# Integer additions moved to VectorE, the first block's second product in float32, and an elu without ScalarE's ReLU

## The chip, the cores and the metric

The kernel runs on one core of a Trainium2 chip. The metric is the device time in microseconds (us) of one execution. A core has five engines that run side by side, each through its own instructions in a fixed order: TensorE (PE; its weight loads are shown as PEld), VectorE (DVE), ScalarE (ACT), GpSimd (POOL) and SyncE (SP), which here only issues DMAs. Engines wait for each other through semaphores, and an instruction that waits holds up all that stand behind it on its engine.

## The reference

Three stages follow each other: a local and block attention, a feed-forward layer with elu, and a mixture of experts.

```python
x = attention(q, k, v)                  # 1536 tokens x 512
h = x @ w_in                            # w_in 512 x 2048
g = where(h > 0, h, exp(min(h, 0)) - 1) # elu
x = g @ w_out                           # w_out 2048 x 512
logits = x @ w_gate                     # 8 experts, the largest is taken
out[mask] = gate * eom * (relu(x[mask] @ w1[e]) @ w2[e])
```

The change touches only the middle lines: how w_in and w_out are converted, how elu is computed, and how `g @ w_out` is multiplied for the first tokens.

## The kernel before

**Blocks and chunks.** The 1536 tokens are worked in four blocks of 512, 256, 384 and 384 tokens (`UNITS`, in units of 64). For each block j the feed-forward layer goes through 16 chunks c of 128 of its 2048 inner columns. `mm_h` makes h of chunk c in a PSUM bank (twelve matmuls, L422), `elu` makes g from it, and `mm_y` adds g times the chunk's rows of w_out into the block's y (L467, one output tile for each 128 tokens). A step of the loop in `part1` emits `mm_h` of its chunk, then `elu`, then `mm_y` of the chunk two steps back, so on PE the order is h of c, y of c-2, h of c+1, y of c-1, h of c+2, y of c.

**Two forms of a product.** In most chunks both factors are split into a high and a low part of type float32r and multiplied with three matmuls for a tile: `split_w` makes the parts of w_out (`wsp`: a cast on ACT at L175, a subtraction on DVE at L176), `split_g` those of g (`gh` on ACT at L447, `gl` on DVE at L448). In the first block's chunks below `C3` (8 before) both splits are left out, and one matmul in float32 stands for a tile (each shows as two matmul records).

**Elu.** `elu` has two instructions of ACT on h, tanh(h/2) into `elt` (L433) and exp(h) into `ele` (L434), and a third, the ReLU of h into `elp` (L435). DVE then makes (exp + 1) * tanh, which is exp(h) - 1, at L436, and min(that, 0) + ReLU at L437. The PSUM banks of h come from the pool `psh`, which has two: h of chunk c+2 can start only when the last reader of h of chunk c is through.

**Conversion.** The weights w_in and w_out come as 64 bit numbers in 32 pieces (16 chunks, two weights each), and the kernel turns each into float32: `conv_r` on ACT rounds the lower word (L127), `conv_t` makes the float's bits from the upper word with two instructions of DVE (L138, L139), and `conv_f` adds the two as integers on POOL (L146). For w_in a split follows: `conv_h` on ACT (L152) and `conv_l`, a subtraction on DVE, or on POOL for three of the sixteen chunks (`LOE`, L157). Seven pieces are converted in `start_up`, whose order is written out in `START`; the other 25 are converted during the first block, two for each step.

**What sets the order.** Apart from `start_up` and the last stage, a scheduler orders each engine's instructions by its own costs and priorities. The attention of a later block's units (L309 to L405) is worked in between the chunks. The pools `gp` (`gh`, `gl`), `ws` and `stg` are rings of a few buffers.

Of the kernel before, what the change touches and what calls it, by code (L numbers as in the profile page):

```python
# [9 lines left out]
F32 = mybir.dt.float32  # L10
# [4 lines left out]
AF = mybir.ActivationFunctionType  # L15
ALU = mybir.AluOpType
# [19 lines left out]
BLK = [j for j in range(NBLK) for _ in range(UNITS[j])]  # L36
NF = FF // 128
NS = 6
C3 = 8
WARM = 22  # L40
AT0 = (2, -2, 1)
ATS = (5, 4, 5)
# [14 lines left out]
EXD = (3, 5)  # L57
EXP = (0, 1, 2, 3, 4, 6, 7)
NORMD = (0, 4, 7)
LOE = "VVVPVV"  # L60
START = "w23 w43 x3 w53 w03 w13 w33 w51 x1 w31 w21 w11 w41 w01 w52 x2 w22 w02 w12 w42 w50 x0 w00 w20 w32 d2 d0 w40 d5 k2 s0 w30 d3 k4 k1 k3 s2 k0 k5 m0 w10 s5 m2 e0 s3 m5 M0 e2 m3 d4 M1 r0 b5 d1 b3 s4 n0 e5 r2 t0 e3 m4 n2 s1 c0 z3 e4 M2 z5 t2 r3 r5 M3 n3 c2 m1 A00 M4 n5 B00 e1 M5 k6 r4 C00 n4 t5 P s6 r1 c5 p1 n1 A01 p6 t4 p2 D0 o5 B01 c4 o2 h5 k7 m6 t3 C01 h2 s7 c3 E0 e6 t1 p7 m7 p0 A10 r6 o0 c1 p3 n6 p4 e7 o3 l5 B10 o1 t6 h3 r7 h0 C10 l3 c6 n7 o4 A11 l0 h1 t7 B20 h4 o6 A20 c7 l1 C20 h6 l4 o7 D1 l2 l6 H0 h7 E1 D2 l7 A30 B30 E2 C30 H1 B11 C11 D3 A21 B21 E3 C21"
HID = (5, 10, 15)
LOP = (1, 3, 5, 8, 10, 12, 14)
# [16 lines left out]
class Prog:  # L80
# [60 lines left out]
    def conv_f(self, c, part):  # L141
        t2, r = self.cv.pop((c, part))
        f = t2
        if part == 1:
            f = self.wo[:, c].bitcast(I32)
        self.nc.gpsimd.tensor_tensor(f, t2, r, op=ALU.add)  # L146
        self.w[c, part] = f

    def conv_h(self, c):
# [4 lines left out]

    def conv_l(self, c):
        w, f = self.w[c, 0], self.cvf.pop(c)
        (self.nc.gpsimd if LOE[c % len(LOE)] == "P" else self.nc.vector).tensor_tensor(w[:, 1], f, w[:, 0].bitcast(F32), op=ALU.subtract)  # L157

    def conv_a(self, c, part):
        self.conv_r(c, part)  # L160
# [8 lines left out]
    def split_w(self, j, c):  # L169
        if j == 0 and c < C3:  # L170
            return
        nc = self.nc
        f = self.w[c, 1].bitcast(F32)
        w = self.ws.tile([128, 2, 512], F32R, tag="ws", name="wsp")
        nc.scalar.copy(w[:, 0], f)  # L175
        nc.vector.tensor_tensor(w[:, 1], f, w[:, 0].bitcast(F32), op=ALU.subtract)  # L176
        self.wsp[j, c] = w
# [247 lines left out]
    def elu(self, j, c):  # L425
        nc = self.nc
        h = self.h.pop((j, c))
        t = self.el.tile([128, TB], F32, tag="t", name="elt", bufs=1)[:, :TBS[j]]
        e = self.el.tile([128, TB], F32, tag="e", name="ele", bufs=1)[:, :TBS[j]]

        pool, tag = (self.gp, "gh" if c % 2 else "gl") if j == 0 and c < C3 else (self.el, "p")
        p = pool.tile([128, TB], F32, tag=tag, name="elp")[:, :TBS[j]]
        nc.scalar.activation(t, h, AF.Tanh, scale=0.5)  # L433
        nc.scalar.activation(e, h, AF.Exp)  # L434
        nc.scalar.activation(p, h, AF.Relu)  # L435
        nc.vector.scalar_tensor_tensor(t, e, 1.0, t, op0=ALU.add, op1=ALU.mult)  # L436
        nc.vector.scalar_tensor_tensor(p, t, 0.0, p, op0=ALU.min, op1=ALU.add)  # L437
        self.g[j, c] = p

    def split_g(self, j, c):  # L440
        nc = self.nc
        if j == 0 and c < C3:
            return
# [13 lines left out]
    def mm_y1(self, j, c, t):  # L457
        nc = self.nc
        g = self.g[j, c]
        sl = slice(t * 128, t * 128 + 128)  # L460
        if j == 0 and c < C3:
            ops = ((g, self.w[c, 1].bitcast(F32)),)
# [74 lines left out]
    def part1(self):  # L537
        nc = self.nc
# [30 lines left out]
        for x in ORDER.split():  # L569
            f = dict(q=self.load_q, n=self.load_v0, v=self.load_v, w=wload, k=self.load_k0, c=self.load_c)[x[0]]  # L570
            f(int(x[1:]))
        self.new_x(0)
        self.new_x(1)
        self.start_up()
        conv_done = [x for x in pieces if x in self.w]
        del cq[:len(conv_done)]
        while dq and dq[0] in self.split:
# [66 lines left out]
        for i in range(len(steps)):  # L644
            run(2 * i)
            j, c = steps[i]
# [19 lines left out]
    def start_up(self):  # L666

        unit = dict(d=self.diag_q, k=self.k_sum, s=self.scores, m=self.maxes, b=self.less_max, e=self.at1b, z=self.sums, r=self.recip, n=self.norm,
                    t=self.turn, c=self.turned, o=self.weighted, h=self.x_hi, l=self.at5, p=self.v_pad, x=self.max_k0, M=self.mean_v0)
        part = dict(A=self.conv_r, B=self.conv_t, C=self.conv_f)  # L670
        self.split, self.half = set(), set()
        with self.tc.manual_schedule():
            for op in START.split():
                if op[0] == "H":
                    self.mm_h(0, int(op[1:]), 0, TB // 2)
                    self.half.add(int(op[1:]))
                    continue
                k, n = op[0], [int(i) for i in op[1:]]
                if k in unit:
                    unit[k](*n)  # L680
                elif k in part:
                    part[k](*n)
                    if k == "C" and n[1] == 1:
                        self.split.add((n[0], 1))
                elif k == "w":
                    self.window(*n)
                elif k == "P":
                    self.pad_v0()
                elif k == "D":
                    self.conv_h(*n)  # L690
                elif k == "E":
                    self.conv_l(*n)
                    self.split.add((n[0], 0))
# [805 lines left out]
```

## Time and profile before

| | |
|---|---|
| time, median of 3 runs | 567.46 us (567.41 to 567.75) |
| profiled execution | 567.08 us |
| its span, first to last instruction | 565.3 us |
| mean granted clock of TensorE | 0.980 of full speed |
| busy: PE, DVE, ACT, POOL | 538.3, 366.3, 311.4, 115.7 us |
| first block's products on PE | about 40 to 172 us |
| last block's products end | about 384 us |

The 1.8 us between the span and the time lie around the program. A busy PE is no proof of PE at its peak, since matmuls are pipelined and a matmul's record is longer than the distance to the next; the distance between two starts is what one costs.

### The profile page before, as it was taken

Reading aid. Unit: us, or ns where it says so; the run is one execution under the profiler, and the core shown is the slowest. Engines: PE = TensorE matmul, PEld = TensorE weight load, DVE = VectorE, ACT = ScalarE, POOL = GpSimd, SP = SyncE. Lnnn points to the kernel's source line nnn. Section 1 sums busy time; section 2 is a strip of 40 time slices with the busy share of each in tenths; the row PEclk is TensorE's granted clock in tenths of the full one; section 3 lists DMA queues with packets and bytes.
Section 4 is the critical chain, followed back from the end, with each engine's and each line's share of the span. In section 5 each row is a group of like instructions: output and inputs, shape, how many; then the busy total and the mean of one; then the engine's idle time right before and its main releaser. Section 6 shows DMA issues by size and latency. Waiting matters only on the chain. (4 is left out here: it accounts for less than half of the span.)

```text
span 565.3 us, 9614 instructions
## 1 busy us (share of the span) xinstructions
PE 538.3 (95%) x3113; PEld 422.5 (75%) x3113; DVE 366.3 (65%) x966; ACT 311.4 (55%) x768; POOL 115.7 (20%) x139
## 2 busy tenths in 40 slices
PE   8877998789999999999999999999999999999995
PEld 4465664557889888988888989877888665675884
DVE  6999899997647886787565778885741100444510
ACT  5775564546557877775665754673232222565620
POOL 3656365434000000000000000431432111100001
PEclk9979999889999999999999999998999999999999
DMA  9999733342114130310100101541077979593611
GB/s 291 317 353 399 239 139 105 123 133 52 57 48 138 49 93 16 118 48 14 48 2 1 56 1 50 170 118 56 19 221 267 382 260 370 162 379 131 237 56 40
DMA packets 38714, 81.33 MB, mean 144 GB/s; under 512 B 4095, under 2 KB 8575, under 8 KB 38656
## 3 DMA queue, kind: packets, MB, share of 16 engines
q1 hardware_dynamic: 36336, 73.30, 38.8%
q0 software_dynamic: 2320, 7.34, 3.8%
q8 instruction: 26, 0.43, 0.3%
q14 instruction: 32, 0.26, 0.1%
HBM read 103.70 MB, written 6.55 MB: 195 GB/s over the span
## 5 line engine op out<-in xcount | busy, mean ns | idle before, releaser
L422 PE MATMUL h<-xh,wi 128*128 128x384 f32 (+2 forms) x528 | 144.6, 342 | 0.2 <-ACT elp L435 0.2
L467 PE MATMUL y<-wsp,gh 128*128 128x512 f32 x320 | 100.9, 403 | 0.3
L422 PEld LDWEIGHTS h<-xh,wi 128*128 128x128 f32 x528 | 93.6, 189 | 8.3 <-ACT elp L435 1.0
L422 PE MATMUL h<-xl,wi 128*128 128x384 f32 (+2 forms) x264 | 88.0, 333 | 0.0
L467 PEld LDWEIGHTS y<-wsp,gh 128*128 128x128 f32 x320 | 58.2, 191 | 10.5 <-ACT gh L447 1.1
L467 PE MATMUL y<-wsp,gl 128*128 128x512 f32 x160 | 62.3, 405 | 1.3 <-DVE gl L448 1.3
L1157 DVE TENSOR_TENSOR holdl<-S,holdh 128x512 fp32r<-128x512 f32 x22 | 15.2, 689 | 72.1 <-ACT holdh L1153 53.7
L1125 PE MATMUL h<-w2s,holdh 128*128 128x512 f32 x176 | 61.0, 407 | 0.0
L1168 PE MATMUL y<-w2s,holdh 128*128 128x512 f32 x176 | 59.1, 398 | 0.0
L436 DVE SCALAR_TENSOR_TENSOR elt<-ele,elt 128x384 f32<-128x384 f32 (+2 forms) x64 | 41.3, 646 | 19.5 <-ACT ele L434 19.1
L422 PEld LDWEIGHTS h<-xl,wi 128*128 128x128 f32 x264 | 49.9, 189 | 4.5 <-issue 1.2
L433 ACT ACTIVATE elt<-h 128x384 f32<-128x384 f32 (+2 forms) x64 | 31.4, 491 | 28.5 <-PE h L422 23.0
L447 ACT CAST gh<-elp 128x384 fp32r<-128x384 f32 (+2 forms) x56 | 27.8, 496 | 31.9 <-DVE elp L437 22.0
L176 DVE TENSOR_TENSOR wsp<-wo,wsp 128x512 fp32r<-128x512 f32 x56 | 39.9, 713 | 8.2 <-ACT wsp L175 7.5
L437 DVE SCALAR_TENSOR_TENSOR elp<-elt,elp 128x384 f32<-128x384 f32 (+2 forms) x64 | 41.8, 652 | 3.9
L175 ACT CAST wsp<-wo 128x512 fp32r<-128x512 f32 x56 | 34.7, 620 | 15.4 <-PE y L467 13.8
L1125 PEld LDWEIGHTS h<-w2s,holdh 128*128 128x128 f32 x176 | 33.9, 192 | 8.3 <-issue 0.8
L336 ACT ACTIVATE e<-e,nb 128x120 f32<-128x120 f32 x88 | 33.7, 389 | 10.4 <-DVE nb L324 10.2
L1168 PEld LDWEIGHTS y<-w2s,holdh 128*128 128x128 f32 x176 | 33.1, 188 | 8.4 <-issue 1.6
L448 DVE TENSOR_TENSOR gl<-elp,gh 128x384 fp32r<-128x384 f32 (+2 forms) x56 | 31.0, 554 | 12.1 <-ACT gh L447 10.8
L467 PEld LDWEIGHTS y<-wsp,gl 128*128 128x128 f32 x160 | 29.9, 190 | 8.4 <-DVE gl L448 2.5
L1125 PE MATMUL h<-w2s,holdl 128*128 128x512 f32 x88 | 35.0, 398 | 0.0
(290 smaller groups left out, 973.1 us busy)
## 6 DMA issues: line engine op xcount, KB each, us to landing
wo<-in_w SPq DMA_DIRECT2D x9, 2048.0 KB
wo<-in_w SPq DMA_DIRECT2D x18, 1024.0 KB
ri<-in_w_in SPq DMA_DIRECT2D x16, 512.0 KB
ro<-in_w_out SPq DMA_DIRECT2D x16, 512.0 KB
wo<-in_w SPq DMA_DIRECT2D x32, 256.0 KB
w2p<-in_w SPq DMA_DIRECT2D x32, 256.0 KB
w2q<-in_w SPq DMA_DIRECT2D x24, 256.0 KB
q<-in_q SPq DMA_DIRECT2D x18, 256.0 KB
```

The lines of the kernel that those rows point to most:

```text
L175: nc.scalar.copy(w[:, 0], f)
L176: nc.vector.tensor_tensor(w[:, 1], f, w[:, 0].bitcast(F32), op=ALU.subtract)
L336: nc.scalar.activation(e[:, p], e[:, p], AF.Exp, bias=nb[:, p:p + 1], scale=0.125, accum_out=sm[:, p:p + 1])
L422: nc.tensor.matmul(h, lhsT=w[:, wl, k * 128:k * 128 + 128], rhs=x[:, k, a:b], start=(n == 0), stop=(n == 11))
L433: nc.scalar.activation(t, h, AF.Tanh, scale=0.5)
L436: nc.vector.scalar_tensor_tensor(t, e, 1.0, t, op0=ALU.add, op1=ALU.mult)
L437: nc.vector.scalar_tensor_tensor(p, t, 0.0, p, op0=ALU.min, op1=ALU.add)
L447: nc.scalar.copy(gh, p)
L448: nc.vector.tensor_tensor(gl, p, gh.bitcast(F32), op=ALU.subtract)
L467: nc.tensor.matmul(self.y[j][t], lhsT=gx[:, sl], rhs=wx, start=(c == 0 and n == 0), stop=(c == NF - 1 and n == len(ops) - 1))
L1125: nc.tensor.matmul(self.h[s, hf], lhsT=x[:, k], rhs=w, start=(n == 0), stop=(n == 11))
L1168: nc.tensor.matmul(self.y2[s], lhsT=g[:, ks], rhs=w, start=(i == 0 and n == 0), stop=(i == 7 and n == 2))
```

## The change

`C3` goes from 8 to 16, so that the whole first block takes the float32 form of `mm_y` and has no splits of w_out and g. `conv_f` adds on DVE once `start_up` is over, and `conv_l` always subtracts on DVE. `elu` has no ReLU: DVE's second instruction reads h itself, max(min(expm1(h), 0), h).

```diff
-C3 = 8
+C3 = 16
...
-LOE = "VVVPVV"
...
-        self.nc.gpsimd.tensor_tensor(f, t2, r, op=ALU.add)
+        (self.nc.gpsimd if self.early else self.nc.vector).tensor_tensor(f, t2, r, op=ALU.add)
...
-        (self.nc.gpsimd if LOE[c % len(LOE)] == "P" else self.nc.vector).tensor_tensor(w[:, 1], f, w[:, 0].bitcast(F32), op=ALU.subtract)
+        self.nc.vector.tensor_tensor(w[:, 1], f, w[:, 0].bitcast(F32), op=ALU.subtract)
...
-        nc.scalar.activation(p, h, AF.Relu)
         nc.vector.scalar_tensor_tensor(t, e, 1.0, t, op0=ALU.add, op1=ALU.mult)
-        nc.vector.scalar_tensor_tensor(p, t, 0.0, p, op0=ALU.min, op1=ALU.add)
+        nc.vector.scalar_tensor_tensor(p, t, 0.0, h, op0=ALU.min, op1=ALU.max)
...
+        self.early = False
...
-        self.split, self.half = set(), set()
+        self.split, self.half, self.early = set(), set(), True
```

The lines of the changed kernel below are up to two lower than before (L434 and L435 are the two instructions of elu on DVE, L145 the integer addition, L421 and L465 the two products).

On DVE, at the first chunk's elu just behind `start_up`, before the change (L436 and L437 are elu, L138 and L139 the conversion, L319 the scores of an attention unit):

```order
L138 TENSOR_SCALAR cv_t<-ro_197 128x512
L139 SCALAR_TENSOR_TENSOR cv_t<-ro_197,cv_t 128x512
L138 TENSOR_SCALAR cv_t<-ro_699 128x512
L436 SCALAR_TENSOR_TENSOR elt<-ele,elt 128x512
L139 SCALAR_TENSOR_TENSOR cv_t<-ro_699,cv_t 128x512
L319 ISA e,mx<-S,mask 128x120
...
L437 SCALAR_TENSOR_TENSOR elp<-elt,elp 128x512
```

and in the changed kernel at the same place:

```order
L138 SCALAR_TENSOR_TENSOR cv_t<-ro_197,cv_t 128x512
L156 TENSOR_TENSOR wi_655<-cv_t,wi_655 128x512
L137 TENSOR_SCALAR cv_t<-ro_699 128x512
L434 SCALAR_TENSOR_TENSOR elt<-ele,elt 128x512
L318 ISA e,mx<-S,mask 128x120
...
L137 TENSOR_SCALAR cv_t<-ri_701 128x512
L435 SCALAR_TENSOR_TENSOR elp<-elt,h 128x512
L145 ISA wo<-cv_t,cv_r 128x1024
```

The subtraction of chunk 3 (L156) now stands ahead of elu on DVE, elu's second instruction reads h, and the first integer addition stands behind it.

On DVE in the middle of the first block, in the changed kernel (one chunk's elu and what stands between its two instructions):

```order
L137 TENSOR_SCALAR cv_t<-ro_938 128x512
L137 TENSOR_SCALAR cv_t<-ri_940 128x512
L138 SCALAR_TENSOR_TENSOR cv_t<-ro_938,cv_t 128x512
L138 SCALAR_TENSOR_TENSOR cv_t<-ri_940,cv_t 128x512
L434 SCALAR_TENSOR_TENSOR elt<-ele,elt 128x512
L145 ISA wo<-cv_t,cv_r 128x1024
L156 TENSOR_TENSOR wi_1082<-cv_t,wi_1082 128x512
L145 ISA cv_t<-cv_t,cv_r 128x1024
L435 SCALAR_TENSOR_TENSOR elp<-elt,h 128x512
```

The 25 additions that stood on POOL stand here. An addition is one instruction over 1024 halves of 16 bits, which are the 512 words of a piece.

On PE, `mm_y` of the first chunk that had the split form, before:

```order
L467 MATMUL y<-wsp,gh 128x512 x2
L467 MATMUL y<-wsp,gl 128x512
L467 MATMUL y<-wsp,gh 128x512
L371 MATMUL T<-c_128,e 120x128 x4
L467 MATMUL y<-wsp,gh 128x512
```

and a chunk of the same part of the block in the changed kernel:

```order
L421 MATMUL h<-xh_201,wi_1144 128x512
L465 MATMUL y<-wo,elp 128x512 x4
L370 MATMUL T<-c_128,e 120x128 x4
L421 MATMUL h<-xh_201,wi_1192 128x512
```

Four matmuls in float32 stand for twelve in float32r.

## Rows read from the trace of the kernel before

**Rows 1.** The page: the engines' busy time and share of the span.

```profile
PE 538.3 (95%) x3113; PEld 422.5 (75%) x3113; DVE 366.3 (65%) x966; ACT 311.4 (55%) x768; POOL 115.7 (20%) x139
```

**Rows 2.** Windows: each engine's busy time by stretch, and the granted clock.

```profile
core 0: us, PE busy (x) PEld busy (x) DVE busy (x) ACT busy (x) POOL busy (x), PEclk, DMA share, GB/s
40.00:60.00 20.00, 16.84 (x90) 12.59 (x88) 19.55 (x34) 11.95 (x28) 13.01 (x11) 0.90 1.03 377
60.00:90.00 30.00, 30.00 (x142) 19.37 (x141) 27.80 (x52) 15.75 (x34) 13.83 (x10) 1.00 0.49 173
90.00:140.00 50.00, 40.97 (x177) 27.96 (x177) 46.22 (x77) 29.26 (x66) 22.96 (x18) 0.93 0.33 100
140.00:360.00 220.00, 220.00 (x1490) 195.11 (x1490) 158.35 (x491) 146.41 (x398) 7.95 (x13) 1.00 0.17 54
360.00:384.00 24.00, 23.70 (x114) 19.24 (x112) 20.97 (x39) 16.06 (x35) 7.57 (x6) 1.00 0.39 111
```

**Rows 3.** Timeline of PE in block 0: start, length, instruction, count, [wait before].

```profile
47.07 0.47 PE L422 MATMUL h<-xh,wi 128*128 128x512 f32 x1
...
53.24 5.37 PE L467 MATMUL y<-wo,elp 128*128 128x512 f32 x8 [3.16 <-DVE elp L437]
...
75.75 3.59 PE L467 MATMUL y<-wo,elp 128*128 128x512 f32 x8
79.18 1.05 PE L309 MATMUL S<-k,q 128*128 128x120 f32 x8
...
101.28 0.65 PE L371 MATMUL T<-c,e 128*120 128x128 f32 x4 [4.40 <-DVE xl L405]
...
126.52 0.40 PE L422 MATMUL h<-xh,wi 128*128 128x512 f32 x1
...
129.27 0.61 PE L467 MATMUL y<-wsp,gh 128*128 128x512 f32 x2
```

**Rows 4.** DVE's groups by line and shape: count, busy us, mean ns of one.

```profile
L176 DVE TENSOR_TENSOR wsp<-wo,wsp 128x512 fp32r<-128x512 f32 x56 | 39.9, 713 | 8.2 <-ACT wsp L175 7.5
L437 DVE SCALAR_TENSOR_TENSOR elp<-elt,elp 128x512 f32<-128x512 f32 x16 | 17.2, 1075 | 0.9
L436 DVE SCALAR_TENSOR_TENSOR elt<-ele,elt 128x512 f32<-128x512 f32 x16 | 15.3, 956 | 2.7 <-ACT ele L434 2.5
L157 DVE TENSOR_TENSOR wi<-cv_t,wi 128x512 fp32r<-128x512 f32 x13 | 14.7, 1133 | 0.1
L138 DVE TENSOR_SCALAR cv_t<-ro 128x512 int32<-128x512 int32 x16 | 12.0, 747 | 3.2 <-POOL wi L157 3.2
L436 DVE SCALAR_TENSOR_TENSOR elt<-ele,elt 128x256 f32<-128x256 f32 x16 | 6.7, 420 | 4.2 <-ACT ele L434 4.1
L138 DVE TENSOR_SCALAR cv_t<-ri 128x512 int32<-128x512 int32 x16 | 6.6, 415 | 0.0
L405 DVE TENSOR_TENSOR xl<-T,xh 128x256 fp32r<-128x256 f32 x16 | 6.6, 413 | 0.9 <-ACT xh L398 0.9
```

**Rows 5.** Timeline of ACT and DVE up to the first chunk's elu.

```profile
45.66 1.66 DVE L139 SCALAR_TENSOR_TENSOR cv_t<-ro,cv_t 128x512 int32<-128x512 int32 x1
45.89 0.60 ACT L434 ACTIVATE ele<-h 128x512 f32<-128x512 f32 x1
48.68 1.79 DVE L436 SCALAR_TENSOR_TENSOR elt<-ele,elt 128x512 f32<-128x512 f32 x1
51.87 1.23 DVE L437 SCALAR_TENSOR_TENSOR elp<-elt,elp 128x512 f32<-128x512 f32 x1
```

**Rows 6.** Timeline of DVE: elu's instructions at two moments of the first block.

```profile
65.38 0.69 DVE L437 SCALAR_TENSOR_TENSOR elp<-elt,elp 128x512 f32<-128x512 f32 x1
...
70.09 1.76 DVE L436 SCALAR_TENSOR_TENSOR elt<-ele,elt 128x512 f32<-128x512 f32 x1
```

**Rows 7.** Timeline of the last block: chunk 12's first product, and chunk 10's elu.

```profile
360.65 0.33 PE L422 MATMUL h<-xh,wi 128*128 128x384 f32 x1
...
361.14 0.55 DVE L437 SCALAR_TENSOR_TENSOR elp<-elt,elp 128x384 f32<-128x384 f32 x1
```

## The prediction

> **What bounds the kernel now.** I read the page's busy times first: PE is busy for 538.3 us, 95% of the span, no other engine for more than 366.3 [rows 1]. PE sets the time, so a change counts where it alters PE's work, or removes or makes time in which PE stands still. The windows say where that is [rows 2]. From 140 to 360 us PE is busy for 220.00 of 220.00 us at a full clock, from 360 to 384 us for 23.70 of 24. There a faster ACT or DVE gains nothing. [...] The clock's share is 0.10 x 20 = 2.0 and 0.07 x 50 = 3.5 us; some 0.3 of the first is the end of a slow stretch from the start, so I count 1.7 + 3.5 = 5.2. DVE in the same stretches is busy for 19.55 of 20 and 46.22 of 50 us: it is what PE waits for. PE's timeline names it too [rows 3]: the first mm_y waits 3.16 us for elu on DVE, a transpose waits 4.40 us for an x_lo of DVE. So the first block is bound by DVE and all else by PE. To be won are 12.2 + 5.2 = 17.4 us at most.
>
> **Why DVE is slow there.** The same instruction of elu takes 0.69 us at 65.38 and 1.76 at 70.09 [rows 6]. The mean of the first block's sixteen is 0.956 for L436 and 1.075 for L437, 1.133 for the thirteen subtractions of L157; L138 takes 0.747 on w_out's pieces and 0.415 on w_in's, for equal shapes [rows 4]. POOL is busy for 13.01, 13.83 and 22.96 us in these three stretches and 7.95 us in the 220 us that follow [rows 2], so I put the excess down to POOL working beside DVE. Its size: 16 x 0.27 + 16 x 0.39 + 13 x 0.44 + 16 x 0.33 = 21.6 us of DVE's time in the first block. With the additions gone from POOL nothing of weight is left on it after start_up.
>
> **The parts.**
>
> *Float32 in the whole first block.* A chunk of four float32 tiles costs PE 79.18 - 75.75 = 3.43 us; twelve float32r matmuls of the same 512 columns cost 129.27 - 126.52 = 2.75 us [rows 3]. Eight chunks cost 8 x 0.68 = **+5.4 us** of PE. DVE loses eight subtractions of 0.71 (L176) [rows 4] and eight of g of about the same length, 11 us; ACT loses sixteen casts, and was at 29.26 of 50 us anyway [rows 2].
>
> *Additions on DVE.* 25 additions and three subtractions come to DVE. A subtraction is 0.69 [rows 6]. The trace has no integer addition on DVE. The row nearest in kind is an elementwise instruction with two inputs over 128x512 words, 0.69. Below: L138 does 512 words in 0.42. Above: the instruction is written over 1024 halves, and from 256 to 512 elements an instruction goes from 0.42 to 0.69 [rows 4, 6], so 1024 would cost 0.69 + 0.54 = 1.23. I take 0.69, as two halves make one word of the usual width, with a chance of about 1 in 6 for 1.23. [...]
>
> *Who sets the pace then.* For a chunk PE does mm_h and mm_y, 2.75 + 3.43 = 6.18 us. DVE does two pieces of conversion (0.42 + 0.69 + 0.69 each), one subtraction (0.69) and elu (2 x 0.69): 5.67 us. The attention units add to both and I count them as equal. DVE is ahead by 0.5 us for a chunk, and for the 12.5 chunks that 25 pieces make, by 6 us. So PE becomes the bound in the first block, narrowly, and the waits from 90 to 140 us go, with the slow clock behind them. I leave 1.0 us of them. The additions wait for conv_r on ACT and for conv_t on DVE itself; behind an addition on DVE stand the next elu and subtraction, but weights are converted some chunks ahead of mm_h, so a late one costs only through elu.
>
> *Elu without the ReLU.* ACT loses 64 instructions and was no bound. DVE's count is the same, and I price reading h from PSUM at nothing: L405, with one input in PSUM, takes 0.413 us for 256 elements and L436 with both in SBUF 0.420 [rows 4]. [...] But the bank of h is now freed by DVE's second instruction, no longer by ACT. That matters at the start. Today mm_h of chunk 2 starts at 47.07 [rows 3], since ACT has read the bank by then; exp of chunk 0 ends at 46.49, but DVE begins elu at 48.68 and its second half at 51.87, to 53.10 [rows 5], for it has conversion and scores ahead. Then mm_y of chunk 0 waits until 53.24. After the change chunk 2's mm_h itself needs that second half. On DVE the subtraction of chunk 3 comes ahead of elu (0.69, or 1.5 beside POOL, which still has two of start_up's additions), and elu's own two lose their excess of 1.10 and 0.54. So I put the second half's end at 52.2, about a microsecond sooner. PE then stands still from 47.07 to 52.2, **5.1 us in place of 3.16**, and runs at the lower clock for a while after it as it does today (the 1.7 us from 40 to 60). Behind this wait all of PE is 2 us later and DVE is not, which adds to DVE's lead.
>
> In the later blocks the new release costs only where elu on DVE is late. In the last block mm_h of chunk 12 starts at 360.65 while elu of chunk 10 ends at 361.69 [rows 7], since DVE has routing and expert weights to do there; that is 1.0 us, and in part ACT's relief brings tanh and exp sooner. I put +0.5 for such places.
>
> **The sum**, against the profiled execution's own 567.08 (565.3 of span and 1.8 around it), which lies 0.4 below the median of 567.46: 567.1 - 17.4 (all of the first block's waits and slow clock) + 5.1 + 1.7 (the first wait and its clock) + 1.0 (waits left) + 5.4 (float32) + 0.5 (later blocks) = 563.4. With the 0.4 that is **563.8 us** in the median, 0.6% faster. Between float32's cost and the longer first wait, more than half of the 17.4 is given back.
>
> **Rivals.**
>
> *The addition goes at one half a cycle (1.23 us).* DVE then has 5.67 + 2 x 0.54 = 6.75 us for a chunk to PE's 6.18, and falls behind by 0.57 x 12.5 = 7.1 us; PE's waits for DVE come back, as today. 563.8 - 1 + 7.1 = 570, slower. It decides against the change from about 1.1 us for an addition, where the lag is 4 us and DVE's own waits for ACT come on top. For it: the instruction is shown as 128x1024. Against: nothing in the trace. Chance 0.15.
>
> *The bank of h is late all along.* DVE's second half stands behind conversions, scores and routing in one queue, and each late one stops mm_h, which today no DVE instruction does. If four chunks of the last block lose the 1.0 us [rows 7], and the starts of blocks as much again together, it is 4 us: about 567.5, no change. For it: the 361.69 against 360.65. Against: DVE is busy for only 158.35 of the 220 us before [rows 2]. Chance 0.15.
>
> *DVE gets well ahead.* The first wait is no longer than today's and goes without a stretch of slow clock, and no wait is left: 563.8 - 1.9 - 1.7 - 1.0 = 559. Chance 0.15. For it: ACT is done by 46.49, and only DVE's order keeps elu of chunk 0 back.
>
> **How the numbers follow.** The forecast itself has 0.55, with 561 to 566 as its own range: a wait more or less in the first block, or 0.1 us in the addition's price (25 x 0.1 = 2.5 us). With the faster rival and part of the two slower ones, 8 in 10 lie between 558.5 and 569.5. About 0.2% (1.1 us) is what a measurement of this kernel can tell from no change. Faster than 566.3: the forecast, nearly all of it, and the faster rival, 0.69. Within 0.2%: half of the late bank and a little of the forecast, 0.15. Slower than 568.6: the slow addition and a rest, 0.16.
>
> **What would show it.** In the changed kernel's profile: L145 on DVE at about 0.69 us and elu at 0.69 everywhere after 53 us; PE's wait before mm_h of chunk 2 (L421), released by elp on DVE, of about 5 us, and none before the first mm_y; PE busy for nearly all of 90 to 140 us at a full clock; mm_y of all sixteen chunks 3.43 us apart from what follows; the first block's end some 4 us sooner, and 140 us to the end unchanged in length. The prediction fails if L145 takes 1.2 us, if PE shows waits on elp throughout, or if DVE's instructions stay long with POOL at rest.

## The result, and the profile after

The changed kernel takes **560.39 us** in the median of four executions (559.02 to 562.2), against 567.43 for the kernel before on the same chip: a ratio of **0.988** (95% interval 0.985 to 0.991). It is 1.2% faster. In a second comparison the ratio was 0.991 (0.988 to 0.994). The profiled execution took 560.03 us, 7.05 less than that of before.

The page of the changed kernel, busy times and shares (answers to [rows 1]):

```profile
PE 537.5 (96%) x3081; PEld 414.2 (74%) x3081; DVE 347.0 (62%) x978; ACT 280.9 (50%) x688; POOL 73.4 (13%) x111
```

PE's busy time is nearly the same, so this row alone explains nothing. The windows of the changed kernel, in the stretches of [rows 2], do:

```profile
40.00:60.00 20.00, 14.62 (x82) 12.05 (x80) 19.80 (x41) 11.32 (x26) 6.28 (x6) 0.83 1.04 377
60.00:90.00 30.00, 30.00 (x140) 19.00 (x138) 26.63 (x67) 17.61 (x43) 0.27 (x1) 1.00 0.56 190
90.00:140.00 50.00, 50.00 (x211) 31.97 (x212) 40.10 (x85) 23.42 (x49) 0.94 (x2) 1.00 0.34 106
140.00:360.00 220.00, 219.32 (x1458) 188.81 (x1456) 149.72 (x483) 124.64 (x339) 8.02 (x13) 1.00 0.15 50
360.00:384.00 24.00, 23.14 (x130) 19.79 (x129) 19.30 (x34) 13.72 (x28) 9.05 (x8) 1.00 0.46 143
```

From 90 to 140 us PE is busy throughout at a full clock, where it stood still for 9.03 us at 0.93 before. POOL is all but at rest from 60 us on, and DVE has 9.9 us to spare where it had 3.8. What got worse stands in the first row: PE is busy for 14.62 of 20 us at a clock of 0.83. PE's timeline in the changed kernel shows why (answers to [rows 3]; L421 is mm_h, L465 mm_y):

```profile
46.14 1.05 PE L308 MATMUL S<-k,q 128*128 128x120 f32 x8
52.57 0.77 PE L421 MATMUL h<-xh,wi 128*128 128x512 f32 x1 [5.38 <-DVE elp L435]
...
57.57 1.02 PE L465 MATMUL y<-wo,elp 128*128 128x512 f32 x2
...
113.53 3.59 PE L465 MATMUL y<-wo,elp 128*128 128x512 f32 x8
116.97 0.60 PE L370 MATMUL T<-c,e 128*120 128x128 f32 x4
```

The first wait stands before mm_h of chunk 2, lasts 5.38 us, and the first mm_y behind it waits for nothing. A chunk's four float32 tiles are 116.97 - 113.53 = 3.44 us apart from what follows. DVE around that wait (answers to [rows 5]):

```profile
47.32 0.68 DVE L156 TENSOR_TENSOR wi<-cv_t,wi 128x512 fp32r<-128x512 f32 x1
47.93 1.49 DVE L137 TENSOR_SCALAR cv_t<-ro 128x512 int32<-128x512 int32 x1
49.34 0.74 DVE L434 SCALAR_TENSOR_TENSOR elt<-ele,elt 128x512 f32<-128x512 f32 x1
...
51.75 0.67 DVE L435 SCALAR_TENSOR_TENSOR elp<-elt,h 128x512 f32<-128x512 f32 x1
52.35 0.68 DVE L145 CUSTOM_DVE_ANT_0 wo<-cv_t,cv_r 128x1024 uint16<-128x1024 uint16 x1
```

And DVE's groups from 40 to 166 us, the first block of the changed kernel (answers to [rows 4]):

```profile
L434 DVE SCALAR_TENSOR_TENSOR elt<-ele,elt 128x512 f32<-128x512 f32 x16 | 11.1, 692 | 14.0 <-ACT ele L433 14.0
L435 DVE SCALAR_TENSOR_TENSOR elp<-elt,h 128x512 f32<-128x512 f32 x16 | 10.9, 682 | 0.2
L156 DVE TENSOR_TENSOR wi<-cv_t,wi 128x512 fp32r<-128x512 f32 x15 | 10.3, 686 | 0.8 <-ACT wi L151 0.7
L145 DVE CUSTOM_DVE_ANT_0 wo<-cv_t,cv_r 128x1024 uint16<-128x1024 uint16 x13 | 8.9, 686 | 0.0
L137 DVE TENSOR_SCALAR cv_t<-ro 128x512 int32<-128x512 int32 x15 | 8.5, 566 | 0.0
L145 DVE CUSTOM_DVE_ANT_0 cv_t<-cv_t,cv_r 128x1024 uint16<-128x1024 uint16 x12 | 8.2, 685 | 0.0
L137 DVE TENSOR_SCALAR cv_t<-ri 128x512 int32<-128x512 int32 x13 | 5.5, 421 | 0.0
```

The integer addition costs 0.69 us. Elu's instructions are at 0.69 and 0.68 (0.96 and 1.08 before), the subtraction at 0.69 (1.13), and DVE now waits 14.0 us for exp on ACT: it is ahead.

Why they were longer shows instruction by instruction. Two rows of the kernel before, from its timeline:

```profile
71.26 1.73 POOL L146 TENSOR_TENSOR cv_t<-cv_t,cv_r 128x512 int32<-128x512 int32 x1
...
71.96 1.58 DVE L437 SCALAR_TENSOR_TENSOR elp<-elt,elp 128x512 f32<-128x512 f32 x1
```

Elu's instruction ends at 73.54, POOL's at 72.99: 0.55 us earlier. From 40 to 170 us that trace has 26 instructions of conversion, elu and splits on DVE that are longer than 0.8 us. Every one of them began while POOL had an addition or a subtraction under way. Those with two inputs end 0.55 us after one of POOL's instructions, the shifts on w_out's pieces (L138, one input) 0.28 us after one; that each began its work only there is an inference from these two lengths. Of these kinds no instruction that ran with POOL idle took more than 0.70 us. In the changed kernel three long ones are left, all beside start_up's last additions on POOL. Above 0.69 us (0.42 for the shifts) the 26 held 24.7 us of DVE's time; the three hold 3.1.

### The profile page after: what moved, and what is told of

Read it like the earlier page. It is cut to its first block, busy times and chain, and to the rows that moved or that the text cites. A ratio compares the mean times of both kernels' runs of the same rounds, so it can differ in the third digit from the quotient of the medians.

```text
span 558.3 us, 9381 instructions
## 1 busy us (share of the span) xinstructions
PE 537.5 (96%) x3081; PEld 414.2 (74%) x3081; DVE 347.0 (62%) x978; ACT 280.9 (50%) x688; POOL 73.4 (13%) x111
## 5 line engine op out<-in xcount | busy, mean ns | idle before, releaser
L421 PE MATMUL h<-xh,wi 128*128 128x384 f32 (+2 forms) x528 | 148.5, 348 | 5.7 <-DVE elp L435 5.7
L421 PEld LDWEIGHTS h<-xh,wi 128*128 128x128 f32 x528 | 95.0, 191 | 14.6 <-issue 6.7
L421 PE MATMUL h<-xl,wi 128*128 128x384 f32 (+2 forms) x264 | 88.8, 336 | 0.0
L465 PE MATMUL y<-wsp,gh 128*128 128x512 f32 x256 | 79.9, 399 | 0.0
L434 DVE SCALAR_TENSOR_TENSOR elt<-ele,elt 128x384 f32<-128x384 f32 (+2 forms) x64 | 36.1, 564 | 40.6 <-ACT ele L433 40.2
L465 PE MATMUL y<-wo,elp 128*128 128x512 f32 x128 | 58.6, 595 | 0.0
L421 PEld LDWEIGHTS h<-xl,wi 128*128 128x128 f32 x264 | 50.5, 191 | 5.0 <-issue 2.2
L465 PEld LDWEIGHTS y<-wsp,gh 128*128 128x128 f32 x256 | 46.0, 188 | 7.5 <-ACT gh L445 0.2
L465 PE MATMUL y<-wsp,gl 128*128 128x512 f32 x128 | 49.3, 401 | 0.0
L174 ACT CAST wsp<-wo 128x512 fp32r<-128x512 f32 x48 | 29.7, 619 | 23.0 <-PE y L465 22.7
L465 PEld LDWEIGHTS y<-wo,elp 128*128 128x128 f32 x128 | 23.6, 189 | 22.2 <-issue 21.1
L435 DVE SCALAR_TENSOR_TENSOR elp<-elt,h 128x384 f32<-128x384 f32 (+2 forms) x64 | 35.2, 550 | 1.1
L1167 PE MATMUL y<-w2s,holdl 128*128 128x512 f32 x88 | 34.4, 391 | 0.0
L296 POOL COPY k<-ks 128x96 f32<-128x96 f32 x16 | 7.0, 439 | 208.5 <-PE S L308 128.9
```

The costliest lines, as they stand in the source:

```text
L296: self.nc.gpsimd.tensor_copy(k[:, 0], self.ks[u // UPB])
L421: nc.tensor.matmul(h, lhsT=w[:, wl, k * 128:k * 128 + 128], rhs=x[:, k, a:b], start=(n == 0), stop=(n == 11))
L435: nc.vector.scalar_tensor_tensor(p, t, 0.0, h, op0=ALU.min, op1=ALU.max)
L465: nc.tensor.matmul(self.y[j][t], lhsT=gx[:, sl], rhs=wx, start=(c == 0 and n == 0), stop=(c == NF - 1 and n == len(ops) - 1))
L1167: nc.tensor.matmul(self.y2[s], lhsT=g[:, ks], rhs=w, start=(i == 0 and n == 0), stop=(i == 7 and n == 2))
```

## The experiments

Three parts were changed at once, so the first runs take them apart. Each ratio is against the kernel before on the same chip.

| additions on | float32 chunks | ReLU | median us | ratio, 95% interval |
|---|---|---|---|---|
| DVE | 8 | kept | 551.55, again 552.25 | 0.975 (0.970 to 0.980), 0.974 (0.972 to 0.977) |
| POOL | 16 | kept | 571.99 | 1.009 (1.006 to 1.013) |
| POOL | 8 | none | 565.10 | 0.996 (0.993 to 0.999) |
| DVE | 16 | kept | 560.37 | 0.989 (0.984 to 0.994) |
| DVE | 8 | none | 557.16 | 0.984 (0.980 to 0.987) |
| POOL | 16 | none | 568.58 | 1.004 (1.002 to 1.007) |
| DVE (the change) | 16 | none | 560.39, again 561.04 | 0.988 (0.985 to 0.991), 0.991 (0.988 to 0.994) |

### The additions alone

The kernel before with the diff's edits of `conv_f`, `conv_l` and `early`, and no others.

> The kernel before with one part alone: the 25 additions and the three subtractions go to VectorE. The ReLU stays, and float32 stays with the first eight chunks. Theory (POOL beside DVE makes DVE slow, DVE sets the first block's pace): elu goes back to 0.69 us an instruction, the first wait stays in front of the first mm_y and falls from 3.16 to about 2.4 us, no float32 is paid; but in chunks 8 to 12 DVE has about 7.0 us of work a chunk (5.67 and two split subtractions) to PE's 5.5, so 3 to 7 us of waits come back there: 557 to 561 us. Rival (the dropped splits carry the gain, the additions only move load): waits as before, 566 us or more.

551.55 us: faster than the whole change by 8.8 us, and 5.5 us below the theory's range, so the theory was too slow. The rival falls. The waits that I had expected in chunks 8 to 12 did not come, as this kernel's windows and its PE waits from 40 to 170 us show (us in total, times, longest):

```profile
40.00:60.00 20.00, 17.11 (x93) 13.39 (x89) 17.80 (x38) 11.01 (x26) 8.36 (x13) 0.91 1.03 394
...
90.00:140.00 50.00, 50.00 (x245) 37.47 (x244) 47.60 (x105) 34.59 (x78) 2.83 (x3) 1.00 0.36 115
```

```profile
PE S L308 <- DMA q<-in_q: 2.1, 1, 2.1
PE y L524 <- ACT mab L511: 1.4, 1, 1.4
PE y L466 <- DVE elp L436: 0.8, 1, 0.8
```

The wait at L524 belongs to the routing behind the first block. DVE is busy for 47.60 of 50 us, and that is enough: PE is busy throughout without float32 in the later chunks.

### Float32 in the whole first block alone

```diff
-C3 = 8
+C3 = 16
```

> The kernel before with one part alone: the whole first block's second product in float32. Additions stay on POOL, the ReLU stays. Theory (POOL beside DVE): DVE loses about 11 us of subtractions but its other instructions stay at 0.95 to 1.1 us; PE gets 5.4 us more work. The 9.0 us of waits and 3.5 of clock from 90 to 140 us go in part, about half: 567.4 + 5.4 - 6 = 566 to 567 us. Rival (the dropped splits carry the gain): all of these 12.5 us go, 560 to 561 us, as in the changed kernel.

571.99 us, 4.3 slower than before: 5 us above the theory's range, and further still from the rival. Its PE waits from 40 to 178 us:

```profile
PE T L371 <- DVE xl L405: 5.6, 2, 4.4
PE y L467 <- DVE elp L437: 3.2, 1, 3.2
PE T L392 <- ACT et L378: 1.4, 2, 1.1
PE T L236 <- DVE xl L405: 1.1, 1, 1.1
PE h L422 <- ACT elp L435: 0.2, 1, 0.2
```

That is 11.5 us, where the same view of the kernel before has 12.2 in its first block. Dropping the splits removed 0.7 us of waiting, while PE pays 5.4. DVE's relief comes too late. In the kernel before the first split product of the block (L467, y from wsp) starts at 118.96 us, and 8.9 of the 12.2 us of waits lie ahead of it; the same four waits are here again (3.2, 0.2, 4.4 and 1.1 us). The last of this run's waits ends at 139.91 us, and 12.6 of the 13.2 us that DVE is idle before elu, waiting for exp on ACT, come behind it.

### Elu without the ReLU alone

The kernel before with the diff's two edits of `elu`.

> The kernel before with one part alone: elu without the ReLU. Theory: ACT was no bound, and the bank of h is now freed by a DVE that is late. The first wait moves to mm_h of chunk 2 and lasts from 47.1 to 53.1 us, 6 us in place of 3.16, and more waits on elu's second half come between 90 and 140 us: 570 to 573 us. Rival (the relief of ACT carries the gain): 564 us or less.

565.10 us: neither theory nor rival. The first wait became about as long as I had said, but the block did not end later (172.09 us against 171.79, by the start of its last mm_y). Its PE waits from 40 to 172 us, the two largest:

```profile
PE h L422 <- DVE elp L436: 6.3, 2, 5.6
PE T L371 <- DVE xl L405: 2.5, 1, 2.5
```

PE's waits come to 12.7 us in all, against 12.2 before, so the longer first wait is not added: behind it the wait for xl falls from 5.5 to 2.5 us. Two things can have brought that, and no run parts them. PE's longer wait gives DVE a lead. And elu's second instruction, which now has one input in PSUM, is no longer held up beside POOL. DVE's rows of this run from 40 to 172 us:

```profile
L138 DVE TENSOR_SCALAR cv_t<-ro 128x512 int32<-128x512 int32 x15 | 14.7, 980 | 0.0
...
L436 DVE SCALAR_TENSOR_TENSOR elp<-elt,h 128x512 f32<-128x512 f32 x16 | 10.9, 680 | 0.3
```

Eight of the sixteen began while an addition ran on POOL and none took more than 0.69 us, against a mean of 1.075 before. Other instructions met the additions in its place (the shift on w_out's pieces has 0.980, before 0.765 in the same stretch), and the time above the undisturbed lengths falls only from 24.7 to 20.1 us. Neither my theory nor the forecast had this. Of the 2.2 us between the two profiled executions 1.7 are a stretch at a lower clock at the start of the last stage, which the one of before has (0.86 from 384 to 396 us) and this one has not (1.00 from 320 to 480); the 0.4% in the median is left open.

### The ReLU put back into the changed kernel

```diff
         nc.scalar.activation(e, h, AF.Exp)
+        nc.scalar.activation(p, h, AF.Relu)
...
-        nc.vector.scalar_tensor_tensor(p, t, 0.0, h, op0=ALU.min, op1=ALU.max)
+        nc.vector.scalar_tensor_tensor(p, t, 0.0, p, op0=ALU.min, op1=ALU.add)
```

> The changed kernel with the ReLU put back (additions on VectorE and float32 in the whole first block stay). Theory: ACT frees the bank of h again, so that mm_h of chunk 2 starts at 47.1 us and only the first mm_y waits, 2.4 to 3.2 us in place of 5.4, with a shorter slow clock behind it; nothing else changes: 560.4 - 2.2 to 3.9 = 556.5 to 558.2 us. Rival (the relief of ACT is worth something later): 560 us or slower.

560.37 us, a ratio of 0.989 against 0.988: no difference that can be measured, so by time the rival's number. The trace has the theory's step and something against it. PE's timeline in this kernel:

```profile
49.01 1.14 PE L308 MATMUL S<-k,q 128*128 128x120 f32 x8 [2.27 <-DMA q<-in_q]
49.90 0.70 PE L421 MATMUL h<-xh,wi 128*128 128x512 f32 x1
```

mm_h of chunk 2 starts 2.67 us sooner, and not the theory's 5 us, since here a matmul ahead of it waits 2.27 us for a DMA; the first block ends 3.06 us sooner than in the changed kernel (162.55 against 165.61). But this execution has a stretch at a lower clock at the start of the last stage, and the profiled one of the changed kernel has none. Windows of this kernel, and then of the changed one:

```profile
376.00:384.00 8.00, 7.48 (x45) 6.39 (x44) 4.26 (x15) 2.75 (x6) 1.71 (x3) 0.82 0.28 101
384.00:396.00 12.00, 12.00 (x52) 9.41 (x52) 8.67 (x43) 3.06 (x6) 3.21 (x11) 0.84 0.00 0
```

```profile
376.00:384.00 8.00, 7.49 (x51) 6.04 (x50) 4.28 (x9) 4.06 (x8) 1.71 (x3) 1.00 0.27 100
384.00:396.00 12.00, 12.00 (x63) 9.68 (x62) 10.72 (x55) 3.80 (x8) 3.55 (x11) 1.00 0.00 1
```

That is 0.18 x 8 + 0.16 x 12 = 3.4 us. Of the 3.06 us only 1.55 are left when the last stage starts (381.83 against 383.38), and the slow stretch more than takes these back. Why the medians agree as well is not settled.

### The changed kernel with float32 in eight chunks only

```diff
-C3 = 16
+C3 = 8
```

> The changed kernel with float32 only in the first eight chunks, as before (additions on VectorE and elu without the ReLU stay). Theory (additions carry the gain, float32 is paid on PE): it drops the cost of float32, 5.4 us by the spacing of the matmuls, and keeps all else; against the kernel with the additions alone it has the longer first wait, 2.7 us at most: 552 to 555 us. Rival (DVE needs float32's relief once elu frees the bank of h): waits on elu's second half between 90 and 140 us, 557 us or more.

557.16 us: 2 us above the theory's range and by time the rival's number, 0.4 to 0.7% below the change's two ratios. But the rival's waits are not there. From 40 to 165 us PE waits for elu only once:

```profile
PE h L421 <- DVE elp L435: 5.4, 1, 5.4
PE S L308 <- DMA q<-in_q: 0.3, 1, 0.3
```

Against the kernel with the additions alone, mm_h of chunk 2 starts 4.08 us later (53.25 against 49.17) and the block ends 3.8 us later (161.10 against 157.28). Once PE sets the pace, the longer first wait is paid nearly in full: the theory had it at 2.7 us at most.

### The additions back on POOL

```diff
-        (self.nc.gpsimd if self.early else self.nc.vector).tensor_tensor(f, t2, r, op=ALU.add)
+        self.nc.gpsimd.tensor_tensor(f, t2, r, op=ALU.add)
```

> The changed kernel with the additions back on POOL (float32 in the whole first block, elu without the ReLU and the subtractions on VectorE stay). Theory: DVE's instructions beside POOL are long again and PE's waits between 90 and 140 us are back, while float32's 5.4 us stay: 568 to 572 us. Rival (float32 and elu relieve DVE enough): 563 us or less.

568.58 us, within the theory's range. The long instructions are back: from 40 to 172 us the mean of elu's first on DVE is 0.907 us and that of the subtractions 1.152, and PE stands still for 4.96 of the 50 us from 90 to 140. Elu's second, with h from PSUM, stays at 0.681. Without the additions on DVE the other two parts (with the three subtractions on DVE) make the kernel 0.4% slower: they are not what the change gains by.

### POOL at work beside DVE

The kernel with the additions alone, plus work on POOL that nobody needs:

```diff
+        self.scr = c.tile([128, 256], I32, name="scr")
...
         (self.nc.gpsimd if self.early else self.nc.vector).tensor_tensor(f, t2, r, op=ALU.add)
+        if not self.early:
+            for a in (0, 256):
+                self.nc.gpsimd.tensor_tensor(self.scr, t2[:, a:a + 256], r[:, a:a + 256], op=ALU.add)
```

> The kernel with the additions alone on VectorE, and behind each of the 25 additions POOL adds the same operands once more, as two instructions over 256 words, into a scratch tile that nobody reads. Theory (POOL working beside DVE lengthens DVE's instructions): DVE's elu and subtractions go back from 0.69 to about 1.0 us, DVE is late again, and 9 to 16 us of waits and slow clock come back: 560 to 567 us. Rival (the gain comes from the hand-over, since an addition on POOL takes 1.3 us and two semaphores in the chain from conversion to split): POOL's work waits for nobody, DVE's instructions stay at 0.69 us, 551 to 553 us.

574.97 us (ratio 1.016, 1.012 to 1.021): 23 us slower than the same kernel without the extra additions, more than the theory said, and slower than before. DVE's groups in this kernel from 40 to 170 us, POOL's below:

```profile
L160 DVE TENSOR_TENSOR wi<-cv_t,wi 128x512 fp32r<-128x512 f32 x15 | 13.9, 930 | 0.3
L439 DVE SCALAR_TENSOR_TENSOR elt<-ele,elt 128x512 f32<-128x512 f32 x16 | 13.5, 842 | 0.6 <-ACT ele L437 0.5
...
L440 DVE SCALAR_TENSOR_TENSOR elp<-elt,elp 128x512 f32<-128x512 f32 x16 | 12.5, 784 | 0.3
L146 DVE CUSTOM_DVE_ANT_0 wo<-cv_t,cv_r 128x1024 uint16<-128x1024 uint16 x13 | 11.4, 874 | 0.1
...
L138 DVE TENSOR_SCALAR cv_t<-ri 128x512 int32<-128x512 int32 x13 | 7.5, 574 | 2.9 <-POOL scr L149 2.9
```

```profile
L149 POOL TENSOR_TENSOR scr<-cv_t,cv_r 128x256 int32<-128x256 int32 x50 | 53.4, 1068 | 45.2 <-DVE cv_t L146 31.2 <-DVE rr L357 5.4 <-DVE cv_t L139 4.5
```

In the same stretch of the kernel without the extra work, the same four kinds of instruction take 0.679, 0.691, 0.683 and 0.682 us. The rival falls: nobody uses what POOL makes here, and DVE's instructions grow. From 40 to 170 us 35 instructions of these kinds, conversion and splits are longer than 0.8 us, and each ends 0.55 or 0.28 us after one of POOL's, as in the kernel before. The time of the run does not price this alone. POOL's extra reads also hold the tiles (2.9 us of DVE's waits in the rows above), and other work on POOL comes later (from 90 to 150 us PE waits 2.9 us for a copy there).

### Float32 in four chunks

The kernel with the additions alone, and

```diff
-C3 = 8
+C3 = 4
```

> The kernel with the additions alone on VectorE, with float32 only in the first four chunks in place of eight. Theory (with the additions on DVE, DVE just keeps up, and float32 buys time for it with time of PE): PE saves 4 x 0.68 = 2.7 us, DVE gets eight subtractions of 0.69 us (5.5 us) where it was busy for 28.4 of 30 us; waits of 2 to 6 us come: 551 to 555 us. Rival (PE alone sets the time): 548.8 us.

555.90 us (0.982, 0.978 to 0.986), a little past the end of the theory's range, and the rival falls. Its window from 90 to 140 us:

```profile
90.00:140.00 50.00, 45.55 (x232) 35.17 (x232) 48.22 (x106) 34.92 (x72) 5.54 (x3) 1.00 0.38 115
```

PE stands still for 4.45 us of these 50, more than the 2.7 us of float32 that it saved. Its waits name a copy on POOL (2.2 us) and casts on ACT (1.3 and 1.0), not DVE. ACT is hardly busier than with eight chunks (34.92 against 34.59 us), and DVE is at 48.22 of 50, so which engine is behind these waits is not shown. Of 4, 8 and 16 chunks with the ReLU kept, eight are best by the ratios (0.982, 0.975 and 0.974, 0.989).

### Four kernels side by side

Three comparisons with the changed kernel, on one chip in five rounds. The changed kernel itself:

> The changed kernel itself once more, as the measure for the three that run with it on the same chip: 560 us.

It took 561.04 us (559.96 to 563.98). The ReLU in chunks 0 and 1 of the first block only:

```diff
+        if j == 0 and c < 2:
+            nc.scalar.activation(p, h, AF.Relu)
...
+        if j == 0 and c < 2:
+            nc.vector.scalar_tensor_tensor(p, t, 0.0, p, op0=ALU.min, op1=ALU.add)
+        else:
             nc.vector.scalar_tensor_tensor(p, t, 0.0, h, op0=ALU.min, op1=ALU.max)
```

> The changed kernel with the ReLU put back in chunks 0 and 1 of the first block alone; the order on DVE is the same. Theory (the longer first wait is the whole cost of elu's new form, and the later blocks gain about 1 us by it): ACT frees the bank of h, mm_h of chunk 2 starts at about 47 to 49 us, the first wait is 2.5 to 3 us shorter and the later blocks are as in the changed kernel: 557 to 558 us. Rival (the wait is only moved, and what it costs is had back behind it): 560 us, as the changed kernel.

560.40 us (557.83 to 561.93), ratio 0.989 (0.987 to 0.992): by time not told apart from the changed kernel's 0.991, and so the rival's number and not the theory's 557 to 558. In the traces mm_h of chunk 2 starts at 48.16 us in place of 53.02, and PE waits 2.5 us before the first mm_y in place of 5.5 before mm_h. The first block ends 4.6 us sooner and the first matmul of the last stage starts 2.4 us sooner. So the step is seen, and its 2 us lie within the spread of the executions.

The additions alone, again:

> The kernel before with the additions alone on VectorE, once more, as the measure beside the changed kernel on the same chip. Theory: faster than the changed kernel by float32's 5.4 us and the longer first wait's 2.7 us, less 1 us in the later blocks: 7 us, so 552 to 553 us. Rival (its 551.6 us came from that chip alone): 556 us or more.

552.25 us, 8.8 less than the changed kernel beside it, a little more than expected. And the same with the ReLU left out in the three later blocks:

```diff
+        if j == 0:
+            nc.scalar.activation(p, h, AF.Relu)
...
+        if j == 0:
+            nc.vector.scalar_tensor_tensor(p, t, 0.0, p, op0=ALU.min, op1=ALU.add)
+        else:
+            nc.vector.scalar_tensor_tensor(p, t, 0.0, h, op0=ALU.min, op1=ALU.max)
```

> The kernel with the additions alone on VectorE, with the ReLU kept in the first block and left out in the three later ones. Theory: the first block is that of the kernel with the additions alone, and the three later blocks are 1.0 us shorter, as they were in the profile of each kernel without the ReLU: 550.5 to 551.5 us, the fastest of all. Rival (the later blocks' microsecond comes from work moved across the border of the first block): as the kernel with the additions alone.

551.96 us (0.974, 0.971 to 0.976): not told apart from 552.25. Whether the later blocks gain anything by the new elu stays open. These two are the fastest versions, 1.6% ahead of the changed kernel beside them.

## Why the prediction was right, step by step

The forecast was 563.8 us, faster; measured were 560.4, also faster and within the range, though below the likeliest case's own 561 to 566. The mechanism held and some sizes were off. Of the 3.4 us between them up to 1.7 lie in a stretch of slow clock that one profiled execution has and the other has not (below).

- **PE waits for DVE in the first block, and DVE is slow because POOL works beside it.** Shown. The 17.4 us of the forecast stand in [rows 2]: PE at rest for 3.16 and 9.03 us, and a granted clock that is 0.10 and 0.07 short of 1.00 there (0.50 from 55 to 57 us in the same trace). POOL off: DVE's instructions return to 0.69. POOL on again without use: they grow, to 0.78 to 0.93. And each long one ends 0.55 or 0.28 us after an instruction of POOL. The forecast argued from two rows of which one is L437 and the other L436, not the same instruction, but L437 itself is at 0.69 and at 1.58 us. The excess was 21.6 us by my estimate; counted by instruction it fell from 24.7 to 3.1. The four terms of the estimate give 16 x (1.075 - 0.682) + 16 x (0.956 - 0.692) + 13 x (1.133 - 0.686) + 16 x (0.747 - 0.566) = 19.2 us by the rows of after; L139 on w_in's pieces, which I had left out, and L176 make up the rest. The 0.566 is no price of w_out's pieces: two of these shifts still meet start_up's additions on POOL (1.52 and 1.49 us), the others take 0.42 as on w_in's.
- **The price of an addition, 0.69.** Measured 0.686, so the rival of 1.23 falls.
- **Reading h from PSUM costs nothing.** Shown, and it even gains beside POOL, which was not forecast (0.680 us in the run without the ReLU alone, 1.075 before). Elu's second instruction takes 0.682 us with h in PSUM (after) and 0.683 with both inputs in SBUF (the additions alone).
- **The first wait, 5.1, and its clock, 1.7.** Measured 5.38 before mm_h of chunk 2, with elu's second half ending at 51.75 + 0.67 = 52.42 for a forecast 52.2. The granted clock is 0.50 from 52 to 57 us and 0.88 from 57 to 58. The lower clock went on to 57.2 us, where the distance of PE's matmuls falls from 0.43 to 0.23 us: 0.5 x (57.2 - 52.57) = 2.3.
- **Float32, +5.4.** Eight chunks of 3.44 - 2.75 are 5.5 us. The first block ends 5.3 us later with float32 than without (162.55 against 157.28, both with additions on DVE and the ReLU); without the ReLU it is 4.5 (165.61 against 161.10). It buys nothing here: alone it took away 0.7 us of waits, and without it DVE kept up. That is the step that was off, **"Who sets the pace then"**: I took 5.67 us of DVE for a chunk to 6.18 of PE as a narrow lead that float32 gives, and 7.0 to 5.5 without it as a lag. The working counted the attention units as equal on both, and PE stayed fully busy at eight chunks too. It did not hurt the forecast, since float32 was in the change anyway.
- **Waits left, 1.0, and later blocks, +0.5.** Measured about none: no wait of PE but the first up to 170 us, and for elu 0.4 us from there to 380. The rival of the late bank falls. The rival in which DVE gets well ahead does so in part: DVE is ahead, but not at the first wait.
- **The first block's end, some 4 us sooner.** It was 6.2 (165.61 against 171.79 us, by the start of its last mm_y). By the start of the last stage 5.3 are left (383.38 against 388.70), so what follows the block is not quite unchanged. PE has begun on the second block's products by then (before, L422 on 128x256 at 161.40 us already), so the end of the first does not tell all of its progress; whether that is the 0.9 us is not shown.
- **Not forecast:** the profiled execution of before has a stretch at a lower clock at the start of the last stage, worth 0.14 x 12 = 1.7 us, that of after has none (its row is shown above). The row of before:

```profile
384.00:396.00 12.00, 11.50 (x66) 9.73 (x66) 6.53 (x27) 3.40 (x8) 1.71 (x3) 0.86 0.18 66
```

With the measured sizes the sum is 567.1 - 17.4 + 5.4 + 2.3 + 5.3 - 1.7 = 561.0 for a measured 560.0; the last 1.0 us is not assigned to any step.

The larger lesson is in what the change gave back. The additions alone are worth 15 to 16 us of the 17.4 that before's profile showed to be won. Float32 and the new elu took 8.8 of them, measured side by side on one chip. How the 8.8 divide is not settled: float32 costs 8.8 us with the ReLU (551.55 and 560.37, on one chip) and 0.4 to 0.7% without it, 2 to 4 us, and neither is the 5.5 of PE's time. The clock has a part in it: the mean granted clock of the changed kernel's six executions on that chip was 0.980 to 0.989, of the additions alone 0.988 to 0.994.

## What to carry to other kernels

When an engine's equal instructions differ in length from one stretch to another, look at which engine is at work beside it, and whether the long ones end with that engine's, before counting its load: moving work **onto** the late engine made it faster (25 additions and three subtractions, a ratio of 0.975). A part that trades the time of the bounding engine for that of another must bring its relief where the waits are: float32 paid here in chunks 4 to 7 (0.982 with 4 chunks, 0.975 with 8) and cost more than it brought in chunks 8 to 15 (0.989 with 16), with DVE late as well as ahead. So try the parts of a change apart. A wait at the start of a stretch cost nearly its length where the waiting engine set the pace of what follows (3.8 of 4.1 us here); where the other engine was late, it did not (without the ReLU alone the first wait grew from 3.16 to 5.6 us and all waits from 12.2 to 12.7).

## What the runs showed of the hardware

- From 40 to 170 us fifty additions of 256 words on POOL beside DVE took 1.07 us each, and DVE's instructions with two inputs in SBUF grew by 15 to 37% (0.683 to 0.784, 0.679 to 0.930 us). The integer addition on DVE grew as well, from 0.682 to 0.874.
- The long instructions of DVE end shortly after one of POOL's: in the kernel before all 26 end 0.55 us (two inputs) or 0.28 us (the shift on w_out's pieces) after one. Once POOL's was the longer: at 133.00 us a subtraction of DVE took 0.68 us beside an addition of 2.13, the longest of the 32 on POOL (mean 1.48). Elu's second instruction with h in PSUM was not held: it began ten times while an addition ran on POOL, in two runs, and took 0.67 to 0.69 us, where the form with both inputs in SBUF went up to 1.75.
- Much of the spread between executions went with the granted clock. Of six executions of the kernel with the additions alone, the three at a mean clock of 0.991 to 0.994 took 550.7 to 551.5 us, the three at 0.988 took 553.0 to 553.5. At the start of the last stage a stretch at a lower clock appeared in some traces and not in others (from 384 to 396 us 0.86 in the kernel before and 0.84 with the ReLU put back, 1.00 in the changed kernel), behind the 5.1 to 5.7 us between the last mm_y and that stage's first matmul. What decides it stays open.
